# The second matrix of a fast-multiply MLP: its seven products in two mirrored orders, with fewer sums out of PSUM

## Chip, cores and metric

One core of one Trainium2 chip. The time is device microseconds (us) of one execution of the whole program. In what follows PE is TensorE's matmul, PEld its weight load, DVE is VectorE, ACT ScalarE, POOL GpSimd, and SP SyncE, which issues the DMAs.

## The reference

```python
x = attention(q, k, v)                     # sigmoid attention, 12 heads, 4 x 448 tokens, head size 64
x = gated_mlp(x, w_in, w_spatial, ...)     # to 4 x 448 x 768
xn = (x - mean) / sqrt(var + 1e-06) * g_ln
ch = maximum(xn @ w_ch1, 0) @ w_ch2        # w_ch1 768 x 3072, w_ch2 3072 x 768
out = x + ch
```

All is float32. The change is in the line of `ch`, which fills the program from about 369 us to its end.

## The kernel before

**Products and precision.** Each factor is kept as a high part and a low part, and a product of two blocks is three passes on PE (high by high, high by low, low by high; lines 359 to 361, `mm3`). Both matrices of the MLP are multiplied in Winograd's form: four quadrants of each factor, seven products in place of eight, and sums and differences of quadrants before and behind them. For tokens these are called A11, A12, A22, S1 to S4, for weights 11, 21, 22, T1 to T4, and for the hidden layer H11, H12, H22, S1 to S4.

**Tiling.** The 3072 hidden units are 12 groups. The first half of the stage (cells i = 0 to 11, 512 columns) takes eight chunks of 128 tokens through all 12 groups, the second (i = 12 to 23, 384 columns) the other six. A cell (`Hidden(i)`) has seven P products (w_ch1; each into one of two PSUM banks, the tiles `ps` of the rows) and seven S products (w_ch2; into one of two accumulators `acc[0]`, `acc[1]` of three banks each). Every product is nine groups of matmuls; the program issues them alternately, P(i,0), S(i-1,0), P(i,1), S(i-1,1) and so on. A *slot* is the place behind one product: P(i,k) is slot 14i + 2k, S(i-1,k) the one behind it. `settle(slot)` issues what a table has planned for that slot. What an engine is given stands in its queue in the order of issue.

**From P to S.** `after` takes a finished P product: ACT copies it (`copied`, L1302), or DVE adds it to an earlier one (L1306) and ACT takes the relu (`summed`, L1307). `high` (L1291, ACT) and `low` (L1297, DVE) make the two parts. After A22, ACT makes H21 by a relu from PSUM (L1344), and `s_add` (L1318, DVE) adds H22 and H21 to S1; S2, S4, S3 are three more such adds, each in a later slot.

**From S to the result.** `SEVEN` writes the order of the S products out by hand, for even and odd groups: hidden name, weight name, accumulator, whether the accumulator starts afresh, and which quadrant of the result DVE then adds the whole accumulator to (`add`, L1384, 128x1536). Six of seven products are followed by such a sum. The next product into the same accumulator waits for it.

**Weights.** Groups 0, 1 and 11 are prepared ahead. For groups 2 to 10 they are made in the first half, a group ahead of use: decode on ACT (L405, L410) and DVE (L414), for w_ch2 of the even groups instead a load of decoded values by SP (`load_plain`, L822); the combinations T1 to T4 on POOL (`make`, L829, one 128x384 operation each); the high part on ACT (L834), the low part on DVE or POOL (L837). `W2_JOBS` says in which slots, counted from slot 14(g+1), the first of the next cell, w_ch2's come: a plain name is a split with the low part on POOL, a name with `v` one with the low part on DVE, `=` a `make`. All go out to memory and are only fetched in the second half.

**Around the halves.** During cell 11, POOL and DVE split and combine the six other chunks' tokens (L1420, L1423). The last group's S products run alone, at the end.

Of the kernel before, what the change touches and what calls it, by code (L numbers as in the profile page):

```python
# [99 lines left out]
    {"T1": ((0, 1), (0, 0)), "T3": ((1, 1), (0, 1)), "T2": ((1, 1), (0, 0)), "T4": ((1, 0), (1, 1))},  # L100
# [24 lines left out]
ENDING = [(*t[:4], t[4] or (0, 0)) for t in SEVEN[1]]
LAST = [ENDING[k] for k in (1, 0, 2, 3, 4, 5, 6)]
# [170 lines left out]
def sigmoid_attention_gmlp_mlp(ctx: ExitStack, tc, q, k, v, w_in, w_sp, w_out, g_ln, w1, w2, out):  # L297
# [959 lines left out]
    class Hidden:  # L1257


        def __init__(self, i):  # L1260
            self.i, self.two = i, i >= NGRP
            self.w = weights[i % NGRP]
            self.n = (3 if self.two else 4) * P
            self.r, self.h, self.hb = {}, {}, {}
# [23 lines left out]
        def high(self, name):  # L1288
            b = self.hb[name] = h_free.popleft()
            t = self.h[name] = b.ap(2, 512)[:, :, : self.n]  # L1290
            nc.scalar.copy(t[:, 0], self.rt(name))  # L1291

        def low(self, name, eng=None):
# [3 lines left out]
            (eng or nc.vector).tensor_sub(t[:, 1], self.rt(name), t[:, 0])  # L1297
# [11 lines left out]

        def s_add(self, name, eng=None, low=None):  # L1310
# [4 lines left out]
                "S3": ("H11", "H21", ALU.subtract),  # L1315
# [7 lines left out]
            if name in ("S3", "S4"):  # L1323
                self.drop({"S3": "H11", "S4": "S2"}[name])

        def after(self, x, ps):
# [9 lines left out]
            elif x == "S4":  # L1336
                self.summed("H12", ps)
# [9 lines left out]
        def steps(self):
            if self.i == 2 * NGRP - 1:
                return LAST
            return ENDING if self.i == NGRP - 1 else SEVEN[self.i % 2]  # L1350

        def step(self, k):
            steps = self.steps()
            hn, wn, b, first, out = steps[k]
            if first is None:
                first = self.i % NGRP == 0
# [9 lines left out]
            rest = steps[k + 1 :]  # L1366
            if not any(t[0] == hn for t in rest):
                h_free.append(self.hb.pop(hn))
            if not any(t[1] == wn for t in rest):
                w_free.append(self.w.t.pop((1, wn)))  # L1370
            if out:
                self.add(ps, out)
            if self.i == 2 * NGRP - 1 and not any(t[4] == out for t in rest):
                for j in range(3):
                    self.store(out, j)

        def add(self, ps, out):
# [89 lines left out]
    def at(i, slot):  # L1467
        return 14 * i + slot
# [228 lines left out]
```

## Time and profile before

| | us |
|---|---|
| median of 3 runs (1057.75 to 1057.96) | 1057.89 |
| the profiled execution's own time | 1059.89 |
| its span | 1058.10 |
| PE busy | 1005.4 (95%) |
| DVE busy | 800.6 (76%) |
| ACT busy | 510.8 (48%) |
| POOL busy | 359.7 (34%) |

The span is from the first to the last instruction of the profile; 1.79 us of the profiled time lie around it. Shares are means over the whole program, so the stage's own stretches are what to read.

### The profile page before, as it was taken

How to read it: one execution, taken by the hardware profiler on the slowest of the kernel's cores; microseconds unless marked ns; L12 is line 12 of the kernel's file. 1: busy time of each engine (PE TensorE's matmuls, PEld its weight loads, DVE VectorE, ACT ScalarE, POOL GpSimd, SP SyncE). 2: the span in 40 equal slices, each digit the busy share in tenths (PEclk: the TensorE clock that was granted, in tenths of full speed). 3: DMA queues.
4: the chain of work that ended last, by engine and by line, in shares of the span. 5: the costliest groups of instructions: out<-in, count | busy, mean ns of one | idle time of the engine just before them, and what ended most of it. 6: DMA issues, size and time to landing. Idle time of an engine off the chain costs nothing. (4 is left out here: it accounts for less than half of the span.)

```text
span 1058.1 us, 14729 instructions
## 1 busy us (share of the span) xinstructions
PE 1005.4 (95%) x5140; PEld 823.0 (78%) x5140; DVE 800.6 (76%) x1025; ACT 510.8 (48%) x843; POOL 359.7 (34%) x309
## 2 busy tenths in 40 slices
PE   9999999999899998989999899998899999999996
PEld 5556666678799986866666666766689999999995
DVE  3769897638777866898888888887876778676765
ACT  5766545436766754556465564644422323323331
POOL 4532322111205715366657656565600021000000
PEclk9999999999999998999999999999999999999998
DMA  8866889557873588656657567567788888888883
GB/s 223 240 227 215 299 286 290 210 190 240 304 280 135 193 311 300 240 216 245 250 214 284 199 258 258 220 226 262 246 286 300 284 306 248 248 252 248 250 250 132
DMA packets 98552, 261.01 MB, mean 247 GB/s; under 512 B 13104, under 2 KB 27440, under 8 KB 98352
## 3 DMA queue, kind: packets, MB, share of 16 engines
q1 hardware_dynamic: 93072, 246.67, 69.3%
q0 software_dynamic: 1760, 7.36, 2.0%
q10 hardware_dynamic: 3648, 6.06, 1.7%
q8 instruction: 41, 0.67, 0.3%
q14 instruction: 31, 0.25, 0.1%
HBM read 168.54 MB, written 91.50 MB: 246 GB/s over the span
## 5 line engine op out<-in xcount | busy, mean ns | idle before, releaser
L1384 DVE TENSOR_TENSOR f_all<-acc,f_all 128x1536 f32<-128x1536 f32 (+1 forms) x138 | 214.5, 1555 | 48.8 <-PE acc L361 47.4
L359 PE MATMUL ps<-r_all,t_all 128*128 128x384 f32 (+1 forms) x432 | 158.8, 368 | 4.2 <-DVE f_all L1306 4.2
L360 PE MATMUL ps<-r_all,t_all 128*128 128x384 f32 (+1 forms) x432 | 158.3, 366 | 0.5 <-POOL r_all L1420 0.5
L361 PE MATMUL ps<-r_all,t_all 128*128 128x384 f32 (+1 forms) x432 | 158.5, 367 | 0.0
L1291 ACT CAST r_all<-f_all 128x512 fp32r<-128x512 f32 (+1 forms) x168 | 95.2, 567 | 128.4 <-DVE f_all L1318 126.0
L1297 DVE TENSOR_TENSOR r_all<-f_all,r_all 128x512 fp32r<-128x512 f32 (+1 forms) x167 | 131.5, 788 | 27.9 <-ACT r_all L1291 26.6
L837 POOL TENSOR_TENSOR t_all<-f_all,t_all 128x384 fp32r<-128x384 f32 x86 | 104.0, 1221 | 119.8 <-ACT t_all L834 105.8
L1307 ACT ACTIVATE f_all<-f_all 128x512 f32<-128x512 f32 (+1 forms) x72 | 41.7, 579 | 161.6 <-DVE f_all L1306 161.5
L359 PE MATMUL acc<-r_all,t_all 128*128 128x512 f32 x228 | 92.7, 406 | 16.2 <-ACT t_all L834 14.1
L360 PE MATMUL acc<-r_all,t_all 128*128 128x512 f32 x228 | 91.6, 402 | 8.1 <-DVE r_all L1297 7.8
L359 PE MATMUL ps<-r_all 128*128 128x512 f32 (+2 forms) x249 | 95.1, 382 | 2.2 <-DVE f_all L709 2.2
L361 PE MATMUL acc<-r_all,t_all 128*128 128x512 f32 x228 | 93.1, 408 | 4.0 <-DVE t_all L837 4.0
L829 POOL TENSOR_TENSOR f_all<-f_all 128x384 f32<-128x384 f32 x76 | 91.4, 1211 | 14.1 <-DMA q_all<-xscr 10.3
L1318 DVE TENSOR_TENSOR f_all<-f_all 128x512 f32<-128x512 f32 (+1 forms) x95 | 73.9, 778 | 26.6 <-ACT f_all L1344 26.2
L360 PE MATMUL ps<-r_all 128*128 128x512 f32 (+2 forms) x249 | 93.5, 376 | 0.0
L361 PE MATMUL ps<-r_all 128*128 128x512 f32 (+2 forms) x249 | 93.5, 376 | 0.0
L359 PEld LDWEIGHTS ps<-r_all,t_all 128*128 128x128 f32 x432 | 81.6, 189 | 15.3 <-DVE f_all L1306 4.2
L360 PEld LDWEIGHTS ps<-r_all,t_all 128*128 128x128 f32 x432 | 81.7, 189 | 10.4 <-POOL r_all L1420 1.2
L361 PEld LDWEIGHTS ps<-r_all,t_all 128*128 128x128 f32 x432 | 81.6, 189 | 9.1
L516 ACT ACTIVATE f_all<-ps,bias_s 128x896 f32<-128x896 f32 x70 | 68.1, 1006 | 36.0 <-PE ps L542 16.1
L359 PE MATMUL acc<-t_all,r_all 128*128 128x384 f32 x225 | 76.5, 340 | 4.3 <-issue 4.3
L361 PE MATMUL acc<-t_all,r_all 128*128 128x384 f32 x225 | 76.2, 339 | 0.0
(199 smaller groups left out, 2022.0 us busy)
## 6 DMA issues: line engine op xcount, KB each, us to landing
t_all<-wscr SPq DMA_DIRECT2D x179, 384.0 KB, 3.8
wscr<-t_all SPq DMA_DIRECT2D x122, 384.0 KB, 2.9
q_all<-in_w SPq DMA_DIRECT2D x42, 768.0 KB, 5.4
wscr<-r_all SPq DMA_DIRECT2D x46, 384.0 KB, 3.7
r_all<-wscr SPq DMA_DIRECT2D x31, 384.0 KB, 3.8
m_all<-in_v SPq DMA_DIRECT2D x24, 256.0 KB, 3.3
yscr<-f_all SPq DMA_DIRECT2D x14, 384.0 KB, 2.8
f_all<-in_k SPq DMA_DIRECT2D x45, 112.0 KB, 4.2
```

The costliest lines, as they stand in the source:

```text
L359: nc.tensor.matmul(ps, lh, rh, start=first, stop=False, skip_group_check=skip)
L360: nc.tensor.matmul(ps, lh, rl, start=False, stop=False, skip_group_check=skip)
L361: nc.tensor.matmul(ps, ll, rh, start=False, stop=last, skip_group_check=skip)
L516: nc.scalar.activation(af, ps[:, :, :S], AF.Sigmoid, bias=bias_s, scale=1.0 / math.sqrt(D))
L829: eng.tensor_sub(self.f(m, WHERE[m][name]), self.f(m, a), self.f(m, b))
L837: low.tensor_sub(t[:, 1], x, t[:, 0])
L1291: nc.scalar.copy(t[:, 0], self.rt(name))
L1297: (eng or nc.vector).tensor_sub(t[:, 1], self.rt(name), t[:, 0])
L1307: nc.scalar.activation(t, t, AF.Relu)
L1318: (eng or nc.vector).tensor_tensor(self.rt(out), self.rt(a), self.rt(b), op=op)
L1384: nc.vector.tensor_add(t, x, t)
```

## The change

The seven S products are renamed P1, P2, Q1, Q2, Q3, Q4, Q7. Odd groups issue them as P1 Q1 Q2 Q4 Q3 P2 Q7 into accumulators 0 1 0 1 0 1 0, even groups the other way round, as P2 Q7 Q3 Q4 Q2 P1 Q1 into 1 0 1 0 1 0 1. So the last two products of a group go to the same accumulators, and the same quadrants, as the first two of the next, which accumulate on without a sum between. A small planner (`sums_of`) works out when DVE must add an accumulator out, and may leave products in it that belong to one quadrant more, which is then subtracted: five sums a group, seven for groups 11 and 23 (146 sums in all before, 124 after). One of an even group's five is a subtraction.

S1 and S3 are made by DVE straight from A22's PSUM bank (`s_first`), so H21 is no longer made, but in the last group. H12 is summed in its PSUM bank (`summed_there`), and its high part, relu and low part read that bank. S3 changes sign, and T3 with it. In even groups the order in which S3, S2 and S4 are finished follows the new order of products. `W2_JOBS` of the even groups begins three slots earlier and brings T4 forward; the loads by `load_plain` come two slots earlier; of odd groups only T3, 21 and T4 move. In the last cell P4, P5 and P6 come one S product sooner. PE has the same matmuls.

```diff
-SEVEN = [
...
+USES = dict(
+    P1=("H11", "11"), P2=("H12", "21"), Q1=("S1", "T1"), Q2=("S2", "T2"), Q3=("S3", "T3"), Q4=("S4", "22"), Q7=("H22", "T4")
+)
+ADDS = dict(
+    P1=((0, 0), (0, 1), (1, 0), (1, 1)), P2=((0, 0),), Q1=((0, 1), (1, 1)), Q2=((0, 1), (1, 0), (1, 1)),
+    Q3=((1, 0), (1, 1)), Q4=((0, 1),), Q7=((1, 0),),
+)
+ODD = [("P1", 0), ("Q1", 1), ("Q2", 0), ("Q4", 1), ("Q3", 0), ("P2", 1), ("Q7", 0)]
+EVEN = [("P2", 1), ("Q7", 0), ("Q3", 1), ("Q4", 0), ("Q2", 1), ("P1", 0), ("Q1", 1)]
+LAST = [ODD[k] for k in (1, 0, 2, 3, 4, 5, 6)]
 W2_JOBS = [
     [
-        (-2, "21v"), (-2, "11v"), (-1, "=T1"), (0, "T1v"), (0, "22v"), (0, "=T3"), (1, "=T2"), (2, "T2v"),
-        (4, "T3"), (5, "=T4"), (6, "T4"),
+        (-5, "11v"), (-4, "=T1"), (-3, "22v"), (-3, "21v"), (-3, "=T3"), (-2, "=T2"), (-1, "=T4"), (0, "T4v"),
+        (1, "T3"), (2, "T2"), (3, "T1"),
     ],
     [
-        (-2, "11v"), (-1, "=T1"), (0, "T1v"), (0, "22v"), (0, "=T3"), (1, "=T2"), (2, "T2v"), (4, "T3"),
-        (6, "21"), (7, "=T4"), (8, "T4"),
+        (-2, "11v"), (-1, "=T1"), (0, "T1v"), (0, "22v"), (0, "=T3"), (1, "=T2"), (2, "T2v"), (3, "T3"),
+        (3, "21"), (4, "=T4"), (5, "T4"),
     ],
 ]
...
+        def summed_there(self, name, ps):
+            t = self.rt(name)
+            nc.vector.tensor_add(ps, t, ps)
+            self.high(name, ps)
+            nc.scalar.activation(t, ps, AF.Relu)
+            self.ps[name] = ps
...
+        def s_first(self, ps):
+            t = self.rt("H22")
+            nc.vector.scalar_tensor_tensor(t, ps, 0.0, t, op0=ALU.max, op1=ALU.add)
+            self.r["S1"] = self.r.pop("H22")
+            self.high("S1")
+            t = self.new("S3")
+            nc.vector.scalar_tensor_tensor(t, ps, 0.0, self.rt("H11"), op0=ALU.max, op1=ALU.subtract)
+            self.high("S3")
...
             elif x == "S4":
-                self.summed("H12", ps)
+                self.summed_there("H12", ps)
...
+                old = set(ADDS[p])
+                new = set(ADDS[seq[n + 1][2]]) if n + 1 < len(seq) else set()
+                keep = bool(new) and len(old ^ new) <= len(old)
+                sums = [(o, 1) for o in sorted(old - new if keep else old)]
+                sums += [(o, -1) for o in sorted(new - old)] if keep else []
+                sums_of[i, k] = fresh, sums
+                fresh = not keep
...
-    tokens.append([("S", 2 * NGRP - 1, k) for k in range(7)])
+    i = 2 * NGRP - 1
+    tokens[i] = [
+        *tokens[i][:7], ("P", i, 4), ("S", i - 1, 3), ("P", i, 5), ("S", i - 1, 4), ("P", i, 6), ("S", i - 1, 5),
+        ("S", i - 1, 6),
+    ]
+    tokens.append([("S", i, k) for k in range(7)])
...
-                plan(at(g, t) - 3, lambda f=f, g=g: weights[g].load_plain(f, dec[2 + f]))
+                plan(at(g, 6 + 2 * f), lambda f=f, g=g: weights[g].load_plain(f, dec[2 + f]))
```

**DVE in cell 6, an even group, from H12's sum to S2's add.** Before, in this order: H12's sum, a sum of an accumulator, H22's sum, the lows of H12 and H22, S1's add, an accumulator, S1's low, the lows of w_ch2's 21 and 11, S2's add.

```order
L1306 TENSOR_TENSOR f_all<-f_all,ps_3324 128x512
L1384 TENSOR_TENSOR f_all<-acc,f_all 128x1536
L1306 TENSOR_TENSOR f_all<-f_all,ps_3323 128x512
L1297 TENSOR_TENSOR r_all<-f_all,r_all 128x512 x2
L1318 TENSOR_TENSOR f_all<-f_all 128x512
L1384 TENSOR_TENSOR f_all<-acc,f_all 128x1536
L1297 TENSOR_TENSOR r_all<-f_all,r_all 128x512
L837 TENSOR_TENSOR t_all<-f_all,t_all 128x384
L837 TENSOR_TENSOR r_all<-f_all,r_all 128x384
L1318 TENSOR_TENSOR f_all<-f_all 128x512
```

Now, over the same products: H12's sum into its bank, an accumulator, H22's sum, the two lows (H12's from PSUM), the low of w_ch2's 11, S1 and S3 from PSUM, the lows of 22 and 21, the lows of S1 and S3, an accumulator, S2's add.

```order
L1309 TENSOR_TENSOR ps_3324<-f_all,ps_3324 128x512
L1399 TENSOR_TENSOR f_all<-acc,f_all 128x1536
L1303 TENSOR_TENSOR f_all<-f_all,ps_3323 128x512
L1290 SCALAR_TENSOR_TENSOR r_all<-ps_3324,r_all 128x512
L1294 TENSOR_TENSOR r_all<-f_all,r_all 128x512
L825 TENSOR_TENSOR t_all<-f_all,t_all 128x384
L1334 SCALAR_TENSOR_TENSOR f_all<-ps_3323,f_all 128x512
L1338 SCALAR_TENSOR_TENSOR f_all<-ps_3323,f_all 128x512
L825 TENSOR_TENSOR t_all<-f_all,t_all 128x384 x2
L1294 TENSOR_TENSOR r_all<-f_all,r_all 128x512 x2
L1399 TENSOR_TENSOR f_all<-acc,f_all 128x1536
L1322 TENSOR_TENSOR f_all<-f_all 128x512
```

A sum of an accumulator between S1 and its low is gone, S3 stands beside S1, and 11's low stands ahead of S1.

**ACT at the same place.** Before: H12's relu and high, splits of w_ch2's T4 of group 5 and of w_ch1's 11 of group 7, H22's relu and high, w_ch1's 21, H21's relu, S1's high, and only then w_ch2's 21 and 11 of group 6 (the last two rows).

```order
L1307 ACTIVATE f_all<-f_all 128x512
L1291 CAST r_all<-f_all 128x512
L834 CAST t_all<-f_all 128x384 x2
L1307 ACTIVATE f_all<-f_all 128x512
L1291 CAST r_all<-f_all 128x512
L834 CAST t_all<-f_all 128x384
L1344 ACTIVATE f_all<-ps_3323 128x512
L1291 CAST r_all<-f_all 128x512
L834 CAST t_all<-f_all 128x384
L834 CAST r_all<-f_all 128x384
```

Now: H12's high and relu from its bank, w_ch1's 11 and w_ch2's 11 (the first pair of splits), H22's relu and high, w_ch1's 21, w_ch2's 22 and 21 (the second pair), the highs of S1 and S3.

```order
L1283 ACTIVATE r_all<-ps_3324 128x512
L1311 ACTIVATE f_all<-ps_3324 128x512
L822 CAST t_all<-f_all 128x384 x2
L1304 ACTIVATE f_all<-f_all 128x512
L1281 CAST r_all<-f_all 128x512
L822 CAST r_all<-f_all 128x384
L822 CAST t_all<-f_all 128x384 x2
L1281 CAST r_all<-f_all 128x512 x2
```

All three quadrants of w_ch2 are split ahead of S1's high rather than behind it.

**DVE at the end, cell 23's last hidden parts.** Before: S1's add and low, H11's sum and its low, an accumulator (the one of S(22,6)), the adds of S2 and S4, a low, an accumulator.

```order
L1318 TENSOR_TENSOR f_all<-f_all 128x384
L1297 TENSOR_TENSOR r_all<-f_all,r_all 128x384
L1306 TENSOR_TENSOR f_all<-f_all,ps_3323 128x384
L1297 TENSOR_TENSOR r_all<-f_all,r_all 128x384
L1384 TENSOR_TENSOR f_all<-acc,f_all 128x3x384
L1318 TENSOR_TENSOR f_all<-f_all 128x384 x2
L1297 TENSOR_TENSOR r_all<-f_all,r_all 128x384
L1384 TENSOR_TENSOR f_all<-acc,f_all 128x3x384
```

Now: S1's add, an accumulator of an earlier product, H11's sum, the lows of H11 and S1, the adds of S2 and S4, a low, an accumulator.

```order
L1322 TENSOR_TENSOR f_all<-f_all 128x384
L1399 TENSOR_TENSOR f_all<-acc,f_all 128x3x384
L1303 TENSOR_TENSOR f_all<-f_all,ps_3323 128x384
L1294 TENSOR_TENSOR r_all<-f_all,r_all 128x384 x2
L1322 TENSOR_TENSOR f_all<-f_all 128x384 x2
L1294 TENSOR_TENSOR r_all<-f_all,r_all 128x384
L1399 TENSOR_TENSOR f_all<-acc,f_all 128x3x384
```

The sum between H11's low and the adds of S2 and S4 is gone.

## Rows read from the trace of the kernel before

**Rows 1.** The page, part 1: busy us, share, instructions.

```profile
PE 1005.4 (95%) x5140; PEld 823.0 (78%) x5140; DVE 800.6 (76%) x1025; ACT 510.8 (48%) x843; POOL 359.7 (34%) x309
```

**Rows 2.** Windows: length, busy PE, PEld, DVE, ACT, POOL, clock, DMA share, GB/s.

```profile
430.99:449.81 18.82, 18.82 (x82) 15.26 (x81) 15.71 (x15) 10.43 (x19) 6.55 (x6) 0.95 0.69 247
447.73:719.13 271.40, 246.93 (x1009) 185.46 (x1008) 231.47 (x218) 149.98 (x268) 166.48 (x137) 0.95 0.64 238
514.85:549.62 34.77, 30.92 (x127) 23.16 (x126) 29.71 (x28) 18.91 (x34) 19.46 (x18) 0.95 0.56 213
549.62:583.34 33.72, 31.06 (x128) 23.11 (x126) 29.09 (x28) 19.63 (x35) 23.49 (x19) 0.95 0.74 270
719.13:753.69 34.56, 30.60 (x127) 23.27 (x126) 29.78 (x28) 16.24 (x26) 25.69 (x20) 0.95 0.76 255
753.69:795.74 42.05, 38.27 (x193) 32.37 (x192) 33.26 (x37) 11.01 (x19) 5.81 (x5) 0.91 0.80 270
795.74:1034.51 238.77, 238.77 (x1361) 238.77 (x1360) 170.59 (x216) 73.96 (x150) 11.56 (x6) 0.95 0.85 264
1034.51:1058.10 23.59, 13.57 (x73) 12.24 (x72) 14.19 (x14) 2.48 (x5) 2.02 (x2) 0.88 0.34 117
```

**Rows 3.** Groups by line and form, 447.73 to 719.13, DVE: busy, mean ns, idle before.

```profile
L1384 DVE TENSOR_TENSOR f_all<-acc,f_all 128x1536 f32<-128x1536 f32 x48 | 84.1, 1752 | 8.9 <-PE acc L361 7.8
L1318 DVE TENSOR_TENSOR f_all<-f_all 128x512 f32<-128x512 f32 x33 | 34.0, 1030 | 5.8 <-ACT f_all L1344 5.8
L1306 DVE TENSOR_TENSOR f_all<-f_all,ps 128x512 f32<-128x512 f32 x24 | 16.2, 675 | 0.7 <-PE ps L361 0.7
```

**Rows 4.** The same view and stretch, POOL.

```profile
L829 POOL TENSOR_TENSOR f_all<-f_all 128x384 f32<-128x384 f32 x63 | 76.0, 1218 | 1.8 <-DVE r_all L837 0.5
```

**Rows 5.** Timeline, cell 5: start, length, instruction, idle before it and releaser.

```profile
512.82 0.45 SPq L822 DMA_DIRECT2D f_all<-wfscr  x1
...
517.91 0.51 ACT L834 CAST t_all<-f_all 128x384 fp32r<-128x384 f32 x1 [2.85 <-DMA f_all<-wfscr]
518.47 0.50 PE L359 MATMUL acc<-r_all,t_all 128*128 128x512 f32 x1 [1.38 <-ACT t_all L834]
...
536.08 1.76 DVE L414 SCALAR_TENSOR_TENSOR f_all<-q_all 128x768 uint32<-128x768 uint32 x1 [0.91 <-POOL f_all L829]
537.77 1.48 DVE L1297 TENSOR_TENSOR r_all<-f_all,r_all 128x512 fp32r<-128x512 f32 x1
539.30 0.50 PE L360 MATMUL acc<-r_all,t_all 128*128 128x512 f32 x1 [1.63 <-DVE r_all L1297]
```

**Rows 6.** Timeline, cell 6.

```profile
550.12 0.62 ACT L1291 CAST r_all<-f_all 128x512 fp32r<-128x512 f32 x1 [1.56 <-DVE f_all L1318]
...
552.34 0.91 ACT L834 CAST t_all<-f_all 128x384 fp32r<-128x384 f32 x2
...
552.88 0.51 PE L359 MATMUL acc<-r_all,t_all 128*128 128x512 f32 x1 [1.01 <-ACT t_all L834]
...
555.14 3.52 POOL L829 TENSOR_TENSOR f_all<-f_all 128x384 f32<-128x384 f32 x3
...
558.17 0.50 PE L359 MATMUL acc<-r_all,t_all 128*128 128x512 f32 x1 [0.70 <-ACT t_all L834]
```

**Rows 7.** Timeline, cells 11 and 12.

```profile
733.96 2.16 DVE L1423 TENSOR_TENSOR q_all<-q_all 128x1152 f32<-128x1152 f32 x1 [1.89 <-POOL r_all L1420]
...
737.58 0.50 PE L360 MATMUL acc<-r_all,t_all 128*128 128x512 f32 x1 [1.23 <-DVE r_all L1297]
...
759.54 1.36 DVE L1423 TENSOR_TENSOR f_all<-f_all 128x1152 f32<-128x1152 f32 x1 [1.86 <-POOL r_all L1420]
...
764.48 0.59 PE L359 MATMUL ps<-r_all,t_all 128*128 128x384 f32 x1 [2.21 <-DVE f_all L1306]
```

**Rows 8.** Timeline, the end.

```profile
1037.23 1.34 DVE L1384 TENSOR_TENSOR f_all<-acc,f_all 128x1152 f32<-128x1152 f32 x1
...
1038.68 0.42 PE L359 MATMUL acc<-t_all,r_all 128*128 128x384 f32 x1 [2.45 <-issue]
```

More of the change, by code (lines that the diff above doesn't have):

```diff
@@ L1314, in s_add @@
                 "S4": ("H12", "S2", ALU.subtract),
-                "S3": ("H11", "H21", ALU.subtract),
+                "S3": ("H21", "H11", ALU.subtract),
             }[name]
@@ L1342, in after @@
                     self.low("H22")
-            else:
+            elif self.order is LAST:
                 nc.scalar.activation(self.new("H21"), ps, AF.Relu)
                 self.s_add("S1")
[L1347 to L1350, printed above, removed]
+            else:
+                self.s_first(ps)
         def step(self, k):
[L1353 to L1356, printed above, removed]
+            p, b = self.order[k]
+            hn, wn = USES[p]
+            first, sums = sums_of[self.i, k]
             ps, h, blk = acc[b], self.h[hn], self.w.t[1, wn]
@@ L1365, in step, with add @@
                     mm3(ps[:, j], w[:, 0, j], w[:, 1, j], h[:, 0], h[:, 1], first, True, True)
[L1366 to L1377, printed above, removed]
+            h_free.append(self.hb.pop(hn))
+            w_free.append(self.w.t.pop((1, wn)))
+            for out, sign in sums:
+                self.add(ps, out, sign)
+                left[self.two, out] -= 1
+                if self.two and not left[self.two, out]:
+                    for j in range(3):
+                        self.store(out, j)
+        def add(self, ps, out, sign):
             u, s = out
@@ L1382, in add @@
                 t, x = sums_t[:, u, s], ps.rearrange("p j n -> p (j n)")
-            if (self.two, out) in touched:
+            if (self.two, out) not in touched:
+                touched.add((self.two, out))
+                if sign > 0:
+                    nc.vector.tensor_copy(t, x)
+                else:
+                    nc.vector.tensor_scalar(t, x, -1.0, None, op0=ALU.mult)
+            elif sign > 0:
                 nc.vector.tensor_add(t, x, t)
             else:
-                touched.add((self.two, out))
-                nc.vector.tensor_copy(t, x)
+                nc.vector.tensor_sub(t, t, x)
         def store(self, out, j):
@@ L1398, in sigmoid_attention_gmlp_mlp @@
     hidden = [Hidden(i) for i in range(2 * NGRP)]
+    sums_of, left = {}, {}
+    for two in range(2):
+        for bank in range(2):
+            seq = [
+                (i, k, p) for i in range(two * NGRP, (two + 1) * NGRP) for k, (p, b) in enumerate(hidden[i].order) if b == bank
+            ]
+            fresh = True
+            for n, (i, k, p) in enumerate(seq):
+                old = set(ADDS[p])
[5 more added lines that the diff above has]
+                fresh = not keep
+                for o, _ in sums:
+                    left[bool(two), o] = left.get((bool(two), o), 0) + 1
     def park_turn(i, copy):
@@ L1635, in sigmoid_attention_gmlp_mlp @@
                     cell.low("S3", G)
+            elif k == 0 and cell.order is EVEN:
+                cell.s_add("S2")
             elif k == 1:
```

58 lines of the change are left out of this document (25 added, 33 removed).

## The prediction

> **What bounds the kernel now.** I read the busy shares first: PE works for 95% of the span, the next engine, DVE, for 76% [rows 1]. That leaves PE's idle time and little else, so the second view is the windows, to see where that idle time lies [rows 2]. The second half of the MLP (795.74 to 1034.51) has none: PE and PEld are busy for all of its 238.77 us. Taking sums from DVE there can move nothing, and fewer sums are at most a relief of a queue that nobody waits for. In the first half the same row type reads otherwise. From 430.99 to 449.81 nine products run without a wait, 2.091 us each, so a cell's fourteen cost 29.28 us. The eight cells from 447.73 to 719.13 would take 234.2; they take 271.40. Those 37.2 us are waits. I split them by cell: four cells in which an even group's S products run (34.77 for cell 5, excess 5.49, as one of four that sum to 20.35), and four with an odd group's (33.72 for cell 6, excess 4.44, one of four that sum to 16.8). Cell 11 has 34.56 - 29.28 = 5.28 more; cell 12's window has 42.05 - 38.27 = 3.8 us of idle, and its clock of 0.91 against 0.95 stretches the busy 38.27 by some 1.6, 5.4 in all; the end has 10 us of PE idle in 23.59.
>
> The third view is the timeline at those waits, to see who is late. **Even groups**: PE waits 1.38 us for w_ch2's 21, split by ACT at 517.91, which had itself waited 2.85 us for a load that SP issued only at 512.82 [rows 5]. Then it waits for T1 and T2, which POOL makes from these, and at 539.30 for 1.63 us for S3's low, which stood on DVE behind a decode (L414, 1.76 us) that had waited for POOL. **Odd groups**: at 552.88 PE waits 1.01 us for 11's split on ACT; ACT was late because S1's high had waited 1.56 us for S1's add, and because decodes stand between [rows 6]. The next wait (0.70 for T1) follows the three makes on POOL. DVE is busy for 231.47 of 271.40 us there, 85% [rows 2], so a late release finds a queue; but in each wait above the first cause is another one.
>
> **The change part by part.** *Sums.* One sum fewer a group in the first half takes 1.752 us from DVE [rows 3]. *S1, S3, H12 from PSUM.* S1 and S3 are now made by an operation with one operand in a 512-column PSUM bank and one in SBUF, max and add in one. No such form stands in the trace. Its bounds are 0.675 us (L1306, which has one operand in PSUM) and 1.030 (L1318, both in SBUF) [rows 3]; I take 0.68, since the operands are L1306's. Two adds and one low a group save 3 x 0.35 = 1.1 us more. The add that writes PSUM (H12) has the same two bounds and I take 0.68 again; at 1.03 it costs 0.35 us a group, on an engine that then still has 2.5 us more room. All told DVE's load in a cell falls by 1.75 + 1.05 = 2.8, from about 29 to 26.2 us of 34. ACT loses H21's relu. Both banks are held longer, H12's until H22's sum is done, A22's for two DVE operations; the next product into either comes four products later or more, 8.4 us of cover against some 2 of use, so this costs nothing; without the cover it would be a wait of those 2 us for each.
>
> [...]
>
> *Even groups' weights.* Their loads come two slots (4.2 us) earlier, against a wait of 2.85 on ACT and 1.38 on PE; the splits come three slots (6.3 us) earlier, and all three quadrants before S1. 21 is then done two products before its use, and T1, now the last to be used, six. S3, made next to S1, has five products before its use. So of the waits shown the first, T1's and S3's low go. What is late next is T4, now the second weight in use. I walk POOL's queue from the end of P(i,5): 11's low on DVE ends about 3.5 us behind it; then POOL has eight operations of w_ch2 and of the next w_ch1 (T1, a low, T1, T3, T2, a low, T3, T4) at 1.218 [rows 4], to 13.2; its split on ACT 0.5, to 13.7, if nothing else holds it. PE comes for T4 after six products, at 12.5. I keep 1.5 us a group for this and for the lows of T3 and T2, made by POOL just in time: the walk gives 1.2, and 0.3 for those. Behind T4's split on ACT stand w_ch1's 22 and S2's high, wanted four products later, so a wait of ACT there holds nobody else. Bounds: 0.5 (POOL's operations at 1.1) and 3.5 (11's low one product late). Four groups: 20.35 - 4 x 1.5 = 14.35.
>
> *Odd groups.* 11's split, T1 and T2 keep their slots; the decodes in front of them too, and S3's high takes the place of the relu that went. So the first waits stay. S3's low no longer stands behind a decode, as it did at 537.77 in the even cell; I put that at a tenth of the 4.44, 0.45 us a cell, in three cells: 1.3. Bounds 0 and 8 (half of 16.8, should S1's shorter add, 0.35, and the removed sum ahead of it bring ACT forward by the whole 1.56).
>
> *Cell 11.* No decodes are left, but 25.69 us of POOL [rows 2]. The waits for group 10's weights go as in the other even groups; the one at 737.58 (1.23), a low that stands behind DVE's x_make, itself waiting 1.89 for POOL, stays [rows 7]. 5.28 - 1.8 = 3.5; bounds 2 and 5.
>
> *Cell 12.* DVE waits 1.86 us for POOL's split of the tokens at 759.54, so H11's sum is late and PE waits 2.21 at 764.48 [rows 7], the clock dips to 0.91 in this window. POOL's token jobs queue behind group 10's weights, whose jobs now end about three slots earlier, and DVE has a sum less ahead of that add. Of the 5.4 I take 3, a little over half; bounds 0 and 5.
>
> *The end.* S(22,6) and S(23,0) use one accumulator: PE waits 2.45 us, the DVE sum of 1.34 at 1037.23 in it [rows 8]. Without a sum between, 2.5 us go. S(23,2) still waits for a sum, and the seven final sums stay. Moving the last P products up one step moves no time in a stretch that is all PE. Bounds 1.5 and 3.5.
>
> The sum: 14.35 + 1.3 + 3.5 + 3 + 2.5 = 24.65. On the profiled execution 1059.89 - 24.65 = 1035.2, the span 1.79 less; on the median, 2.0 below that execution, 1057.89 - 24.65 = 1033.2. PE's busy time stays, so all comes out of its idle 1058.10 - 1005.4 = 52.7 us [rows 1].
>
> **Rivals.** *Half of it* (1041 to 1055): the waits are passed on. POOL and ACT hold the weights' chain as before, and T4, T3 and T2 arrive one after the other late in each even group: 3.5 us stay in each (6.4 saved over four), cells 11 and 12 gain 2 and 0, odd groups nothing, the end 2.5. That is 10.9, about 1047. For it: the T waits after 21 in cell 5 were POOL's own. Against: PE had waited for the start of that chain, not for its length. *More* (under 1024): even groups' waits go to nothing (20.35), cells 11 and 12 give 5 each, the odd groups 4 and the end 2.5: 36.9, about 1021. For it: DVE's 2.8 us of relief per cell, where operations with both operands in SBUF may also shrink once it meets POOL less. Against: odd groups' first wait starts on ACT. *No change*: DVE's relief is under a tenth of its load and PE's waits had other first causes, so if the earlier slots only let ACT and POOL wait earlier, the end's 2.5 is all, and odd groups, whose POOL jobs are packed closer, give it back: 1056 to 1060. *Slower*: T4 was the last weight in use and becomes the second. If 11's split, first in the chain, is late by more than PE had before, everything behind it is late: the load by SP stands in a queue behind stores that wait for their data, and ACT had it only at 517.91, 5.1 us after its issue, in the very cell of its use [rows 5]. The gain of 24.65 is used up when T4 comes 24.65 / 5 = 4.9 us later than in my walk in each of five even groups, and the 0.2% bound lies at 5.3. At 6.5 the time is 1057.9 + 5 x 1.6 = 1066. For it: ACT waits for that load now. Against: the loads have 4.2 us more room, and the splits only ask for them 6.3 us earlier, so 2.1 more has to go wrong before anything is later than it was.
>
> **How the numbers follow.** A measurement here tells about 0.2%, 2.1 us. The forecast, 1024 to 1041, has 0.62; half of it 0.17; more 0.10; no change 0.04; slower 0.07. So faster 0.89, same 0.04, slower 0.07. The terms' own bounds move the forecast by some 8 us each way; a range from 1022 to 1048 leaves about 0.06 below it and 0.14 above, and I give it.
>
> **What would show it.** In the profile after: PE idle 28 us rather than 52; the second half's window again all PE and PEld, 238.8; cells 3, 5, 7 and 9 at about 30.8 us rather than 34 and more, with their largest wait at the second S product (T4); cells 4, 6, 8 and 10 within 0.5 us of before; PE without a wait at S(23,0); DVE's busy time some 45 to 55 us less, of which 22 sums make 34 (half of them 1.752, half 1.34); the adds from PSUM at 0.68. I am wrong if T4's wait in even cells is over 3 us, if odd cells fall by 2 us or more, or if cell 12 still dips in clock.

## The result and the profile after

The changed kernel took 1042.51 us (median of 4, 1039.76 to 1044.91) against 1057.93 for the kernel before: ratio 0.9854, 95% interval 0.9828 to 0.9880, 15.4 us faster. The forecast was 1033.2, and the time lies in its range. Measured again over five rounds it took 1041.36 against 1059.85, ratio 0.9831 (0.9810 to 0.9852), 18.5 us.

The page of the changed kernel, part 1, answers to [rows 1]; the windows, with the columns of [rows 2], are those of cells 3 to 10 together, then cells 5, 6, 11, 12, the second half, and the end.

```profile
PE 996.3 (96%) x5140; PEld 824.6 (79%) x5140; DVE 753.9 (73%) x998; ACT 495.7 (48%) x820; POOL 358.2 (35%) x314
```

```profile
447.45:705.58 258.13, 241.85 (x1010) 186.98 (x1008) 208.82 (x208) 144.63 (x259) 167.26 (x143) 1.00 0.67 248
512.07:542.89 30.82, 29.65 (x128) 23.57 (x126) 25.31 (x26) 16.90 (x31) 20.02 (x18) 1.00 0.57 219
542.89:577.10 34.21, 30.86 (x127) 23.14 (x126) 27.64 (x29) 20.32 (x37) 22.34 (x20) 1.00 0.78 288
705.58:737.88 32.30, 29.83 (x127) 23.54 (x126) 27.24 (x25) 14.86 (x24) 23.66 (x20) 1.00 0.89 280
...
777.02:1013.90 236.88, 236.88 (x1350) 236.88 (x1350) 153.56 (x204) 67.48 (x140) 11.65 (x6) 1.00 0.84 264
1013.90:1037.70 23.80, 16.43 (x83) 15.59 (x81) 13.72 (x15) 2.48 (x5) 2.03 (x2) 0.92 0.39 132
```

The eight cells fell from 271.40 to 258.13, DVE's work in them from 231.47 to 208.82. Cell 5, with an even group's S products, went from 34.77 to 30.82; cell 6, an odd group's, from 33.72 to 34.21. The second half is all PE, as before; its window here ends one S product earlier than before's, and its cells 14 to 22 take 22.1 us each in both. PE's idle time fell from 52.7 to 41.4 us. This page shows a granted clock of 1.00 where before's shows 0.95, yet nine undisturbed products take 18.82 us, 2.09 each, in both (430.99 to 449.81 before, 428.63 to 447.45 here); the unchanged code ahead of P(1,0) is 2.9 us shorter in this execution, and that is no work of the change. So cells are compared, from the first matmul of P(i,0) to that of the next cell, and the stretch from P(1,0) to the end. Cells 3, 5, 7 and 9, in which an even group's S products run, are called the even cells from here on, and 4, 6, 8 and 10 the odd ones:

| us, one profiled execution of each | cells 1, 2 | 3, 5, 7, 9 | 4, 6, 8, 10 | 11 | 12 | rest | P(1,0) to end |
|---|---|---|---|---|---|---|---|
| before | 64.3 | 137.5 | 133.9 | 34.6 | 34.4 | 270.0 | 674.7 |
| changed | 66.9 | 122.9 | 135.2 | 32.3 | 31.3 | 268.5 | 657.2 |
| changed, run again | 66.0 | 122.6 | 136.6 | 33.8 | 31.0 | 268.5 | 658.5 |
| six sums a group | 63.9 | 133.4 | 135.1 | 33.8 | 31.0 | 268.8 | 666.0 |
| H21 made again | 65.6 | 126.8 | 142.8 | 33.8 | 32.6 | 268.6 | 670.2 |
| before, weights moved | 66.5 | 141.2 | 137.4 | 38.2 | 32.9 | 270.0 | 686.2 |
| S3's low earlier | 66.4 | 126.0 | 130.5 | 33.8 | 31.0 | 267.0 | 654.8 |
| five moves | 64.1 | 121.2 | 133.1 | 31.2 | 31.0 | 268.5 | 649.1 |
| six moves | 63.4 | 119.6 | 128.8 | 31.2 | 31.0 | 268.5 | 642.5 |

Between the first two rows: -14.5 in even cells, +1.3 in odd ones, -2.3 in cell 11, -3.1 in cell 12, -1.5 in the rest (S(23,0)'s wait is gone, -2.6; the last seven products take 1.1 more), +2.6 in cells 1 and 2, -17.5 in all. The next timelines are of cells 4 and 5 of the changed kernel: the waits that are left.

```profile
498.52 1.76 DVE L402 SCALAR_TENSOR_TENSOR f_all<-q_all 128x768 uint32<-128x768 uint32 x1 [1.89 <-POOL f_all L817]
500.21 1.48 DVE L1294 TENSOR_TENSOR r_all<-f_all,r_all 128x512 fp32r<-128x512 f32 x1
501.74 0.51 PE L348 MATMUL acc<-r_all,t_all 128*128 128x512 f32 x1 [1.69 <-DVE r_all L1294]
...
516.46 1.76 DVE L1399 TENSOR_TENSOR f_all<-acc,f_all 128x1536 f32<-128x1536 f32 x1 [0.18 <-PE acc L349]
518.13 1.50 DVE L1322 TENSOR_TENSOR f_all<-f_all 128x512 f32<-128x512 f32 x1
519.12 0.51 ACT L822 CAST r_all<-f_all 128x384 fp32r<-128x384 f32 x1 [4.18 <-POOL f_all L817]
519.68 0.50 PE L347 MATMUL acc<-r_all 128*128 128x512 f32 x1 [1.17 <-ACT r_all L822]
```

S3's low behind a decode that waited for POOL was an even group's wait [rows 5]; now it is the odd group's, at the fifth S product (501.74). In the even cell PE waits 1.17 us for T4, whose split on ACT waited 4.18 us for POOL.

### The profile page after: what moved, and what is told of

The parts are those of the page before. It is cut to its first block, busy times and chain, and to the rows that moved or that the text cites. A ratio compares the mean times of both kernels' runs of the same rounds, so it can differ in the third digit from the quotient of the medians.

```text
span 1037.7 us, 14773 instructions
## 1 busy us (share of the span) xinstructions
PE 996.3 (96%) x5140; PEld 824.6 (79%) x5140; DVE 753.9 (73%) x998; ACT 495.7 (48%) x820; POOL 358.2 (35%) x314
## 5 line engine op out<-in xcount | busy, mean ns | idle before, releaser
L1399 DVE TENSOR_TENSOR f_all<-acc,f_all 128x1536 f32<-128x1536 f32 (+1 forms) x106 | 164.8, 1555 | 74.6 <-PE acc L349 74.1
L347 PE MATMUL ps<-r_all,t_all 128*128 128x384 f32 (+1 forms) x429 | 157.2, 367 | 1.9 <-DVE f_all L1303 1.9
L349 PE MATMUL ps<-r_all,t_all 128*128 128x384 f32 (+1 forms) x429 | 156.8, 366 | 0.0
L348 PE MATMUL ps<-r_all,t_all 128*128 128x384 f32 (+1 forms) x429 | 156.7, 365 | 0.0
L825 POOL TENSOR_TENSOR t_all<-f_all,t_all 128x384 fp32r<-128x384 f32 x89 | 107.1, 1212 | 96.6 <-ACT t_all L822 70.4
L1281 ACT CAST r_all<-f_all 128x512 fp32r<-128x512 f32 (+1 forms) x144 | 81.4, 567 | 118.4 <-DVE f_all L1322 74.5
L1294 DVE TENSOR_TENSOR r_all<-f_all,r_all 128x512 fp32r<-128x512 f32 (+1 forms) x143 | 112.0, 792 | 34.3 <-ACT r_all L1281 31.7
L347 PE MATMUL acc<-r_all,t_all 128*128 128x512 f32 x222 | 89.1, 402 | 9.9 <-ACT t_all L822 8.4
L348 PE MATMUL acc<-r_all,t_all 128*128 128x512 f32 x222 | 88.0, 397 | 7.5 <-DVE r_all L1294 7.5
L817 POOL TENSOR_TENSOR f_all<-f_all 128x384 f32<-128x384 f32 x76 | 88.4, 1172 | 18.4 <-DVE t_all L825 7.1
L349 PE MATMUL acc<-r_all,t_all 128*128 128x512 f32 x222 | 89.2, 402 | 1.3 <-DVE t_all L825 1.3
L347 PE MATMUL acc<-t_all,r_all 128*128 128x384 f32 x225 | 77.0, 342 | 2.1 <-issue 2.1
L349 PE MATMUL acc<-t_all,r_all 128*128 128x384 f32 x225 | 76.7, 341 | 0.0
L348 PE MATMUL acc<-t_all,r_all 128*128 128x384 f32 x225 | 76.5, 340 | 0.0
L822 ACT CAST t_all<-f_all 128x384 fp32r<-128x384 f32 x120 | 58.5, 510 | 34.5 <-POOL f_all L817 33.5
```

What stands on the lines that cost most here:

```text
L347: nc.tensor.matmul(ps, lh, rh, start=first, stop=False, skip_group_check=skip)
L348: nc.tensor.matmul(ps, lh, rl, start=False, stop=False, skip_group_check=skip)
L349: nc.tensor.matmul(ps, ll, rh, start=False, stop=last, skip_group_check=skip)
L817: eng.tensor_sub(self.f(m, WHERE[m][name]), self.f(m, a), self.f(m, b))
L822: high(t[:, 0], x)
L825: low.tensor_sub(t[:, 1], x, t[:, 0])
```

## The experiments

Each is compared with the kernel before on the same chip, and read beside the changed kernel's 1041.36, which for most of them was measured on another one; a difference to it leaves, by my estimate, 1 to 2 us of doubt (before's medians on the four chips lay between 1059.85 and 1060.73). Timelines and cells are of one execution.

**The changed kernel once more.**

> The changed kernel once more, to see how far its time moves from execution to execution (four executions lay between 1039.76 and 1044.91 us, while before's lay within 0.3 us). If the spread belongs to this kernel, five rounds show 4 to 6 us again, with a median of 1041 to 1044 us; if it was one visit to the chip, they agree within 1 us. The odd cells (4, 6, 8) take 34.2 to 34.6 us with one wait of 1.7 us or more at the fifth S product, the even ones (5, 7, 9) 30.8 to 30.9.

1041.36 us, 1040.98 to 1044.13; cells 5, 7 and 9 at 30.85, 30.82 and 30.52. Before's own times lay between 1057.31 and 1065.33 here, so a spread of some us is not peculiar to this kernel. Cell 8 (36.10 against 34.55) and cell 11 (33.84 against 32.30) show a step of 1.5 us; the last section says what it is.

**Six sums a group.** The planner may not carry an accumulator on from an odd to an even group:

```diff
                 keep = bool(new) and len(old ^ new) <= len(old)
+                keep = keep and not (i % 2 and seq[n + 1][0] > i)
```

> The changed kernel, but an accumulator is added out at each boundary from an odd to an even group, instead of going on: two more DVE sums of 1.75 us at five boundaries of the first half and of 1.34 at five of the second, six sums a group on the mean, as before the change. Theory one: the fewer sums are not what moved the time; these sums have two S products of cover, DVE has room, and the time rises by 0 to 3 us to 1041 to 1045; the second half's cells stay at 22.14 us. Theory two: DVE's queue is what releases the waits in the first half, and each boundary puts its 3.5 us, or most of it, on the path: 10 to 17 us more, with the even cells back at 33 to 34 us.

1053.67 us, ratio 0.9926 (0.9900 to 0.9952): by times and ratios 10 to 12 us of the gain are gone. In the traces the four even cells take 10.5 us more than in the changed kernel's first execution, and the whole stretch 8.8 more. Theory two. The timeline of cell 5 in this kernel:

```profile
519.71 1.75 DVE L1399 TENSOR_TENSOR f_all<-acc,f_all 128x1536 f32<-128x1536 f32 x1
521.38 0.68 DVE L1322 TENSOR_TENSOR f_all<-f_all 128x512 f32<-128x512 f32 x1
521.98 1.35 DVE L825 TENSOR_TENSOR r_all<-f_all,r_all 128x384 fp32r<-128x384 f32 x1
523.38 0.80 PE L349 MATMUL acc<-r_all 128*128 128x512 f32 x1 [1.40 <-DVE r_all L825]
```

```profile
521.25:526.42 5.17, 3.77 (x9) 2.74 (x10) 3.49 (x5) 3.47 (x7) 4.54 (x4) 0.67 0.38 152
```

T4's split was there at 521.19, as late as in the changed kernel; its low (L825) then stood behind a sum and S2's add, and that sum began 1.7 us later in the cell than in the changed kernel, because the two new sums stood ahead of it. PE waited 1.20 and 1.40 us, and the product with these waits ran at a granted clock of 0.67 (the window of its 5.17 us), so the price of a sum here is its own delay and the slow product after it. Cell 3, with waits of 0.81 and 1.40 us and a clock of 1.00 behind them, lost 1.5 us; cells 5, 7 and 9, where the clock fell, lost 2.9 to 3.0 each.

**H21 made again.** S1 and S3 from SBUF, all else as changed:

```diff
         def s_first(self, ps):
-            t = self.rt("H22")
-            nc.vector.scalar_tensor_tensor(t, ps, 0.0, t, op0=ALU.max, op1=ALU.add)
...
+            nc.scalar.activation(self.new("H21"), ps, AF.Relu)
+            self.s_add("S1")
+            self.s_add("S3")
```

> The changed kernel with H21 made again by ACT's relu and S1 and S3 added from SBUF, all else as changed: ACT has 0.6 us more in front of S1's add, and the two adds take 0.68 to 1.5 us in place of 0.68. Theory one: S1's high then comes 0.6 to 1.4 us later on ACT, and 11's split behind it too, so the first wait of the odd groups grows from 0.4 to 1.0 us and more (it was 1.0 before the change); 0.6 to 1.2 us in each of four odd cells, 1 us or less in even ones: 1044 to 1048. Theory two: the bank only saved DVE time that nobody waited for: within 1 us of the changed kernel.

1054.29 us, ratio 0.9934 (0.9912 to 0.9955): 11 to 13 us of the gain are gone, and in the traces the odd cells take 7.6 us more and the even ones 3.9. Theory one, at more than its price. The timeline of cells 3 and 4:

```profile
477.49 0.60 ACT L1333 ACTIVATE f_all<-ps 128x512 f32<-128x512 f32 x1
478.12 2.72 DVE L1322 TENSOR_TENSOR f_all<-f_all 128x512 f32<-128x512 f32 x2
483.03 0.49 ACT L822 CAST r_all<-f_all 128x384 fp32r<-128x384 f32 x1
483.57 0.50 PE L347 MATMUL acc<-r_all 128*128 128x512 f32 x1 [1.95 <-ACT r_all L822]
```

```profile
483.50:487.30 3.80, 3.73 (x10) 2.77 (x11) 2.84 (x3) 1.53 (x4) 3.29 (x3) 0.60 0.17 67
```

A relu of 0.60 and two adds of 1.36 on the mean took the place of two operations of 0.68, and 11's split, behind the two highs and a decode, came at 483.03, 3.65 us behind the cell's start at 479.38; in the changed kernel it came at 479.98, 2.10 behind 477.88. PE waited 1.95 us (0.40 there), and ran the next 3.8 us at a granted clock of 0.60.

**The weights alone.** The kernel before with the slots of the change, and nothing else; the even group's jobs keep their own order:

```diff
-        (-2, "21v"), (-2, "11v"), (-1, "=T1"), (0, "T1v"), (0, "22v"), (0, "=T3"), (1, "=T2"), (2, "T2v"),
-        (4, "T3"), (5, "=T4"), (6, "T4"),
+        (-5, "21v"), (-5, "11v"), (-4, "=T1"), (-3, "T1v"), (-3, "22v"), (-3, "=T3"), (-2, "=T2"), (-1, "T2v"),
+        (1, "T3"), (2, "=T4"), (3, "T4"),
```

> The kernel before, with its own orders, sums and adds, and all the moves of weight jobs that the change makes: even groups' jobs three slots and the loads two slots earlier, and the odd groups' T3, 21 and T4 in the changed kernel's slots, so that the loads no longer meet them. Theory one (the prediction's): the slots alone save most of the even cells' waits, cells 3, 5, 7, 9 fall by 2.5 to 3.5 us to 31 to 32, the time by 8 to 13 us. Theory two (after the runs with six sums and with H21): DVE's and ACT's relief is what lets the earlier weights be in time; without it the splits and lows stand behind sums and adds, and the time falls by less than 3 us or rises.

1070.94 us, ratio 1.0099 (1.0067 to 1.0131): slower than before, with the even cells together 3.7 us longer, the odd ones 3.5, cell 11 3.6 and cells 1 and 2 2.2. Theory two. Cell 5:

```profile
519.66 0.93 ACT L834 CAST t_all<-f_all 128x384 fp32r<-128x384 f32 x2 [2.43 <-POOL f_all L829]
520.49 0.59 ACT L1344 ACTIVATE f_all<-ps 128x512 f32<-128x512 f32 x1
521.12 1.01 DVE L1318 TENSOR_TENSOR f_all<-f_all 128x512 f32<-128x512 f32 x1 [2.64 <-ACT f_all L1344]
...
530.07 0.67 DVE L1306 TENSOR_TENSOR f_all<-f_all,ps 128x512 f32<-128x512 f32 x1
530.79 0.51 PE L359 MATMUL ps<-r_all,t_all 128*128 128x512 f32 x1 [2.02 <-DVE f_all L1306]
```

The earlier split stands on ACT ahead of H21's relu and waits 2.43 us for POOL. DVE waits 2.64 for that relu before it can add S1, everything behind S1 is late, and PE waits 2.02 us at 530.79 for H11's sum, which frees the bank of its next P product. In the changed kernel S1 waits for no ACT operation behind A22's product. This run also keeps the old order of products, so it does not tell that order from the relief of DVE and ACT; and no run has the relief without the earlier slots, so what it gives alone is not shown.

A first form of this run moved the even jobs and the loads, but not the odd groups':

> The kernel before, with its own orders, sums and adds, and only the even groups' weights moved: the jobs of w_ch2 three slots earlier and the two loads two slots earlier. Theory one: the even cells' saving is the weights' earlier slots. The waits for 21, T1 and T2 go, S3's low behind the decode (1.63 us) stays: cells 3, 5, 7 and 9 fall from 34.7 to about 31.5, and the time falls by 10 to 13 us. Theory two: it takes the new orders and DVE's relief; without them the earlier splits stand in the way of other work on ACT and DVE, the loop of GpSimd's operations and loads is no shorter, and the cells fall by 1 us or less: the time falls by less than 4 us.

1068.31 us, ratio 1.0072 (1.0051 to 1.0094). Here the loads overwrite the block from which the odd group's T4 is made, so T4 has other values and its make waits for the load, and the run decides nothing between the theories. The same holds for the changed kernel with the odd jobs put back:

```diff
-        (3, "21"), (4, "=T4"), (5, "T4"),
+        (6, "21"), (7, "=T4"), (8, "T4"),
```

> The odd groups' weight jobs are put back to their old slots (T3 at 4, 21 at 6, T4 at 7 and 8). Theory one: GpSimd's jobs of w_ch2 were moved ahead of w_ch1's T4, whose make frees the block that the decode writes, and so the decode and S3's low behind it came 1.5 us later; with the old slots the odd cells lose that wait and the time falls by 5 to 7 us to about 1036. Theory two: the decode was late before too (S3's low stands behind it wherever the new orders put it), and the odd cells stay at 34.2 us; T4 at slot 8 may then meet the next even group's jobs, which begin at slot 9, and the time stays or rises by 0 to 4 us.

1055.97 us, ratio 0.9963 (0.9948 to 0.9978). Neither theory had the time: the odd jobs were moved to free that block before the loads at slots 6 and 8, and the even cells took 138.1 us in place of 122.9. The odd ones stayed at 135.2, but not with the same waits. At the fifth S product of cell 6 PE waits 0.43 us where it waited 1.71:

```profile
572.67 0.51 PE L348 MATMUL acc<-r_all,t_all 128*128 128x512 f32 x1 [0.43 <-DVE r_all L1294]
```

So the place of POOL's jobs does bear on that wait, as theory one had it, and what it gives comes back at the end of the cell, where the odd group's T4 is now late (the last two products of cells 4, 6 and 8 take 1.0 to 1.7 us more).

**The waits that are left.** S3's low of odd groups one product earlier:

```diff
-            elif k in (1, 2, 3) and prev.order is ODD:
-                prev.low(("S2", "S4", "S3")[k - 1])
+            elif k in (1, 2) and prev.order is ODD:
+                prev.low(("S2", "S4")[k - 1])
+                if k == 2:
+                    prev.low("S3")
```

> In odd groups S3's low is issued one P product earlier, ahead of the decode on DVE. Theory: in the changed kernel the wait of 1.7 to 2.0 us at the fifth S product of each odd group is only that low's place behind the decode, so 4 x 1.7 = 6.8 us go and cells 4, 6, 8 take 32.4 us: 1035.5 us against 1042.5. Rival: DVE is simply behind there, and whatever stands first the next low or sum is late in its place: the time stays within 1.5 us of the changed kernel's, and the wait turns up at the fourth or sixth S product.

1041.51 us, ratio 0.9827 (0.9805 to 0.9848). The theory had the odd cells and the rival the time: cells 4, 6 and 8 fell by some 1.5 us each (32.63 for cell 4), and cells 5, 7 and 9 rose by 1.0, with PE waiting 2.19 us for T4 in place of 1.17. ACT waited 1.70 there for the plain load, which made a suspect:

```diff
-            plan(first, lambda m=m, f=f, w=w, blk=blk: w.load(m, f, blk))
+            plan(max(first, t - 8), lambda m=m, f=f, w=w, blk=blk: w.load(m, f, blk))
```

> The run with S3's low earlier, and beside that only the raw weights' loads not earlier than eight slots ahead of their decode. There the odd cells had gained 1.5 us each and the even ones lost 1.0, where ACT waited 1.7 us for the plain values' load, issued 7.5 us earlier with two raw loads beside it. Theory one: the raw loads made it late; now ACT waits less than 0.6 us, the even cells come back to 30.8 and the odd stay at 32.6: 3 to 4 us less, 1037 to 1038. Theory two: the load is issued late because it stands behind the stores of GpSimd's last pieces, and lands late whatever runs beside it: even cells at 31.8, the time as in that run, 1041.5.

1040.43 us, ratio 0.9805 (0.9775 to 0.9835). ACT's wait for the load was gone, and T4 came as late as in the run before (cell 5, this kernel):

```profile
518.71 0.51 ACT L822 CAST r_all<-f_all 128x384 fp32r<-128x384 f32 x1 [5.19 <-POOL f_all L817]
519.27 0.79 PE L347 MATMUL acc<-r_all 128*128 128x512 f32 x1 [2.20 <-ACT r_all L822]
```

So neither theory: it is POOL's eight operations, from T1's make at 508.88 to T4's split at 518.71, 9.8 us, that PE meets. In the changed kernel they take 9.4 and begin 2.3 us ahead of the cell, here 1.8, which fits a shorter odd cell leaving them less time. Cells 1 and 2 gained from the later raw loads (66.4 to 63.7). T4's make ahead of two of those operations:

```diff
-(-2, "=T2"), (-1, "=T4"), (0, "T4v"),
+(-2, "=T2"), (-2, "=T4"), (0, "T4v"),
```

> The even groups' T4 is made one slot earlier on GpSimd, ahead of two operations for the next group's w_ch1. Theory (the walk of GpSimd's queue in the prediction): T4 comes two operations of 1.0 to 1.5 us earlier, the wait of 1.17 us at the second S product of even groups goes, with its slow restart of 1.3 us in the product before it 1.3 to 1.6 us a group: cells 5, 7, 9 take 29.4 us and the time falls by 5 to 7 us. Rival: T4 waits for T2's make and T1's split, not for its neighbours in the queue, or w_ch1's pieces come late instead: less than 2 us.

1046.13 us, ratio 0.9871 (0.9849 to 0.9893), some 5 us slower than the changed kernel: T4's high was there in time, but its low stood on DVE behind a sum and S2's add until 521.17 and PE waited 2.04 us for it. Neither expected a loss. The restart that the theory counted is smaller, too: in the changed kernel's cell 5 the product ahead of T4's wait took 3.43 us with the wait in it, and the one behind it 2.32, 0.23 more than an undisturbed one. With the split a slot earlier too:

```diff
-(-2, "=T2"), (-1, "=T4"), (0, "T4v"),
+(-2, "=T2"), (-2, "=T4"), (-1, "T4v"),
```

> As in the run with T4 made earlier, but T4's split on ACT also comes one slot earlier, so that its low stands on DVE ahead of the accumulator's sum and of S2's add, behind which it was 2.0 us late. Theory one: this was all that kept the earlier T4 from paying, and now the wait at the second S product of even groups goes: cells 5, 7, 9 at 29.6 to 30.0 us (30.8 in the changed kernel), 4 to 6 us less than it. Theory two: the even groups' weights run in a loop (GpSimd's last operations for an odd group free the block, SP loads the next values, ACT splits, GpSimd makes), which sets the pace of two cells together; what the even cell gains the odd cell or the next even one gives back, and the time is within 2 us of the changed kernel's. ACT's split, waiting for T4, may also hold up H11's copy: up to 1 us a cell more.

1041.78 us, ratio 0.9814 (0.9783 to 0.9846). The wait for T4 is gone, and DVE's order gives it back as 1.07 us for H11's sum, now behind the low, a sum and S2's add; even cells gain 0.3 each. Theory two had the time, but what gives the gain back here is DVE's order.

**Together.** S3's low, T4's make and split, S2's add of even groups behind H11's sum, the raw loads, and the two `x_make` of cells 11 and 12 behind what waited for them:

> The changed kernel with five moves: S3's low of odd groups ahead of the decode; T4 of even groups made and split a slot earlier; S2's add of even groups behind H11's sum; the raw weights' loads not earlier than eight slots ahead of their decode, so that they don't share the DMA queue with the plain loads; the two x_make of cells 11 and 12 behind the low and the sum that waited for them. If the waits are places in a queue, the odd cells keep their 1.5 us, the even ones fall to 29.6 to 30.2 us, cells 11 and 12 lose 2 us each: 1028 to 1034 us. If GpSimd's chain with the loads sets the pace of two cells, the odd cells' gain comes back as T4's wait, and it ends at 1037 to 1041.

1033.61 us, ratio 0.9741 (0.9706 to 0.9776). The time is in the first theory's range, the cells are between the two: even ones at 30.5 (29.6 for cell 3), odd at 33.3, cell 11 at 31.2. Last, the odd groups' first weights one slot earlier:

```diff
-        (-2, "11v"), (-1, "=T1"), (0, "T1v"), (0, "22v"),
+        (-3, "11v"), (-2, "=T1"), (-1, "T1v"), (0, "22v"),
```

> The run with five moves, and odd groups' first piece of w_ch2 (11) split one slot earlier, ahead of S1's and S3's highs and of a decode on ACT, with T1's make and split one slot earlier behind it. Theory one: the waits left in odd cells (1.0 us for 11's split, 0.9 for T1's, with their slow restarts 3 us) are these places in ACT's and GpSimd's queues: cells 4, 6, 8, 10 fall from 33.3 to 30.5 to 31.5, and the time by 6 to 11 us to 1023 to 1028. Theory two: ACT only waits longer for DVE's decode, and S1's high is late in its place: within 2 us of 1033.6.

1028.40 us (1026.51 to 1028.61), ratio 0.9688 (0.9664 to 0.9711), the fastest of all runs. Odd cells took 32.4, 32.3, 31.9 and 32.3, 0.4 to 0.9 us above theory one's range, and the time is 5.2 us less, just outside it. A stretch from its cell 3, to be read against 258.13 with 208.82 of DVE:

```profile
447.65:705.90 258.25, 248.95 (x1052) 195.63 (x1051) 223.26 (x215) 148.74 (x267) 176.93 (x147) 1.00 0.75 263
```

This stretch of the same length holds cells 3 to 10, now 248.4 us, and 9.9 us of cell 11 (from 696.05).

## Why the prediction was right in sign and range, and wrong in part of its cause

*The first half alone.* Right: every gain is there, in cell 12 between the halves, or at the end, and the second half's 22.1 us cells did not move. "PE's busy time stays, so all comes out of its idle" did not hold: PE's idle fell to 41.4 us and not to 28, and in cells 3 to 10 5.1 of the 13.3 us came out of PE's busy time (246.93 to 241.85). The waits here are longer than the idle time shows: matmuls that count 0.39 us each start 0.23 us apart (448.66 and 448.89 before), so the end of the last one covers, by an estimate from these two numbers, some 0.16 us of each wait.

*Even groups, 14.35 of the 24.65.* The measured fall is 14.5, and the wait left is T4's, at the place and, with 1.17 us, at the size of the walk through POOL's queue (1.2). What let the weights be in time is another thing. "In each wait above the first cause is another one" was the step that failed: it put the whole gain down to the weights' slots, and DVE's and ACT's relief at little. The slots alone made the kernel 10 us slower, two sums more at a boundary cost 10 to 12 us, H21's relu with the adds from SBUF 11 to 13. So the slots pay only with the rest of the change: an earlier split on ACT stands in the way where S1 waits for a relu behind it, and T4's low is late where a sum more stands ahead of it. Whether the rest pays without the slots was not run.

*S1, S3, H12 from PSUM.* Grouped by line and form from 447 to 706, the changed kernel's DVE:

```profile
L1294 DVE TENSOR_TENSOR r_all<-f_all,r_all 128x512 fp32r<-128x512 f32 x49 | 51.9, 1066 | 10.6 <-ACT r_all L1281 10.3
...
L1322 DVE TENSOR_TENSOR f_all<-f_all 128x512 f32<-128x512 f32 x16 | 18.8, 1177 | 0.0
...
L1334 DVE SCALAR_TENSOR_TENSOR f_all<-ps,f_all 128x512 f32<-128x512 f32 x8 | 5.5, 688 | 2.8 <-PE ps L349 2.8
L1309 DVE TENSOR_TENSOR ps<-f_all,ps 128x512 f32<-128x512 f32 x8 | 5.5, 687 | 0.2 <-PE ps L349 0.2
L1290 DVE SCALAR_TENSOR_TENSOR r_all<-ps,r_all 128x512 fp32r<-128x512 f32 x8 | 5.5, 682 | 0.0
```

0.68 us each was right, for the add that writes PSUM too. Adds from SBUF (L1322) took 1.18 on the mean: 0.68 where POOL was idle, and 1.18 to 1.51 where POOL worked throughout, where the operations with one operand in PSUM stayed at 0.67 to 0.70. The relief per cell came as forecast (231.47 to 208.82 over eight cells, 2.8 each).

*Odd groups, 1.3 forecast, 1.3 lost (2.7 in the second execution).* The step "S3's low no longer stands behind a decode" failed: it stands there in the odd groups now, and costs 1.7 to 2.0 us. What S1 from the bank gave was 0.6 us at the first wait (1.01 before [rows 6], 0.39 in cell 6). The upper bound of 8 us was not idle: the six moves together took the odd cells 5.1 us below the kernel before.

*Cell 11:* 3.5 forecast, 2.3 in one execution and 0.7 in the other. *Cell 12:* 3 forecast, 3.1 and 3.4, in good part by luck: at H11's sum PE still waits 1.94 us (2.21 before), but the product behind it kept its clock, 1.00 from 747.35 to 751.37 where before's showed 0.57 in the window from 764.48 to 768.50, and waits for POOL's token pieces ahead of it, some 1 us, are gone. In the run with H21 the same wait of 2.21 us kept the clock at 1.00, so the 1.3 us of the slow product are not shown to be the change's. *The end:* 2.5 forecast, 2.6 at S(23,0), of which the last seven products gave back 1.1, at a lower clock behind S(23,2)'s wait (1.88 us, then 0.63 from 1022.37 to 1027.00; before 1.64, then 0.95 from 1043.73 to 1048.36). *Not forecast:* 2.6 us more in cells 1 and 2, 1.7 in the second execution. PE waits there for fetched weights (3.57 us at 413.21 in the first), and the later raw loads took it away; why the loads are late I did not follow further.

The forecast was 24.65; the stretch that the change touches shows 17.5 and 16.2 in two executions, the medians 15.4 and 18.5. The odd cells (2.6 to 4 off), cells 1 and 2 (1.7 to 2.6), the last products (1.1) and cell 11 (1.2 to 2.8) make up the 7 to 8 us. Of the signs of being wrong that the prediction named none came: T4's wait is 1.17 us, the odd cells rose, and cell 12 kept its clock.

## What to carry to other kernels

When a wait has a named releaser, follow what stands ahead of that releaser in its own engine's order of issue; here a split that waited 2.43 us held up a relu, and a sum of 1.75 us held up a weight's low part, and undoing either kind of relief cost more than half of the gain. A part of a change that the profile calls off the path can be what lets another part be in time, so price parts together and test them apart. A low part that is ready early is better issued ahead of an instruction that may wait for another engine: S3's took 1.5 us out of each of three odd cells, which T4's wait gave back until other moves came. Six moves of order and timing, none of which removes work, were worth 13 us more.

## What the runs showed of the hardware

In these runs PE at times paid for a wait twice, in the wait and in a lower granted clock behind it, and the same wait did not always do it. At the same wait of 2.00 us in cell 8, the changed kernel's first execution went on at a clock of 1.00 and the second did not (the first row here is the first execution's):

```profile
632.11 0.50 PE L348 MATMUL acc<-r_all,t_all 128*128 128x512 f32 x1 [2.00 <-DVE r_all L1294]
...
632.79 0.50 PE L348 MATMUL acc<-r_all,t_all 128*128 128x512 f32 x1 [2.00 <-DVE r_all L1294]
```

The window of that S product in each (629.70 in the first, 630.40 in the second):

```profile
629.70:634.10 4.40, 2.40 (x11) 1.64 (x10) 4.40 (x4) 0.32 (x1) 1.56 (x2) 1.00 1.04 312
```

```profile
630.40:635.60 5.20, 3.20 (x10) 2.22 (x9) 5.20 (x5) 0.30 (x1) 1.54 (x2) 0.82 0.97 298
```

And matmuls of the second, before the clock fell and after:

```profile
633.37 0.40 PE L347 MATMUL acc<-r_all,t_all 128*128 128x512 f32 x1
...
634.35 0.63 PE L347 MATMUL acc<-r_all,t_all 128*128 128x512 f32 x1
```

The granted clock was 1.00 through the first and 0.82 on the mean through the second; a matmul went from 0.40 to 0.63 us, and the cell was 1.5 us longer. Cell 11 shows the same step: 32.30 us in the first, where the clock stayed at 1.00 behind a wait of 2.12 us (723.33 to 727.00), and 33.84 in the second. The waits of 1.69 and 1.71 us in cells 4 and 6 left it at 1.00 in the first (498.00 to 506.00, 565.00 to 575.00), and cells 4, 6 and 10 together took no longer in the second, 100.5 us against 100.6. Steps of 1.5 us are of the size of the scatter between executions (1040.98 to 1044.13); that they make most of it is not shown, since other executions have no trace.

DVE's operations on 512 columns with both operands in SBUF took 0.68 to 0.70 us with POOL idle and up to 1.51 beside POOL's, those with one operand in PSUM 0.67 to 0.70 in either case (before and the changed kernel, 370 to 790 us). And the nine products of 18.82 us had a granted clock of 0.95 in before's trace and 1.00 in the changed kernel's. The 2.9 us ahead of P(1,0) do not go with that reading: the last run reads 1.00 there and reaches P(1,0) 0.9 us later than the kernel before.
